# Weights in 16 pieces that alternate with activation tiles in one DMA queue, and an order planned for it

## The chip, the core and the metric

The kernel runs on one core of one Trainium2 chip. The core has a matrix engine (TensorE, PE in the profile; its weight loads are PEld), a vector engine (VectorE, DVE), an activation engine (ScalarE, ACT), GpSimd (POOL) and SyncE (SP). Here SP and POOL mostly issue DMAs: each has a queue of its own, and both queues are served by the same 16 DMA engines. The profile calls SP's queue q1 (hardware_dynamic) and POOL's queue q0 (software_dynamic).

The metric is the device time of one execution in microseconds (us); lower is better. Before the change it was 177.68 us, the median of 3 runs from 177.03 to 177.84.

## What is computed

An RWKV-like linear attention, followed by a two-layer network with squared ReLU. Cut to what matters:

```python
# r, k, v: (4, 8, 768, 48) f32   w, u: (8, 48)   w_in: (384, 2048)   w_out: (2048, 384)
for t in range(S):
    cur = einsum('bhd,bhe->bhde', u * k_t, v_t)
    y_t = einsum('bhd,bhde->bhe', r_t, state + cur)
    state = w[..., None] * state + einsum('bhd,bhe->bhde', k_t, v_t)
x = y.transpose(0, 2, 1, 3).reshape(3072, 384)
h = x @ w_in
out = (relu(h) ** 2) @ w_out
```

## The kernel before

The 768 positions are cut into 6 chunks of 128, and each chunk of each of the 4 batches is a unit: unit i is chunk i // 4 of batch i % 4, 24 units in all. For one unit the steps are these, with the engine that runs each:

- `load:i:rt`, `load:i:kt`, `load:i:vt`: DMAs of the r, k and v tiles, 192 KB each, in rows of 192 bytes. Buffers are taken in turn from small pools (`room`: 3 for r, 8 for k, 4 for v), so a load waits until the buffer's last reader is done.
- `scale:i:0` and `scale:i:1` (DVE): r and k times powers of the decay w, to bf16. `cast_v:i` (ACT): v to bf16.
- `turn:i:0/1` (PE) and `evict_rk:i:0/1` (ACT) transpose both for units 0 to 5; from unit 6 on one transposing DMA of SP's queue does it (`turn_dma:i`).
- `at:i` (PE) multiplies the two; `mask:i:0/1` (DVE) masks the product. `rk:i` (DVE) and `sums:i` (PE) make the diagonal term and the change of the state, `state_add`, `state_decay` (DVE) and `state_cast` (ACT) carry the state.
- `y_mm:i` (PE) and `evict_y:i` (DVE) give the attention's output. It is transposed by `x_turn:i` (PE) and `evict_x:i` (ACT) for units 0 to 5, by `x_dma:i` (SP's queue) after that.
- `mm1:i:m:s` (PE) is the first layer for one unit (m = 1, units 0 to 7) or two (m = 2), for slice s of the 2048 columns; `relu` (ACT) and `square` (ACT or DVE) follow. `mm2:i:q` (PE) is quarter q of the second layer's sum, `evict_o:i` (ACT) and `store:i` write the output.

The weights lie in SBUF in quarters: `w_in_q[0..3]` and `w_out_q[0..3]`, cast from f32 to bf16 by the DMA, which only POOL's queue is used for. A quarter is 768 KB in HBM and 384 KB in SBUF; one DMA brings one quarter (`weights:after:q:I` or `weights:after:q:O`). While units are single, slice s of `mm1` reads quarter s of `w_in` alone; `mm2:i:q` reads quarter q of `w_out` alone.

`fill` is a matmul of ones into a bank that nobody reads (68 of them): it keeps PE occupied where the plan has nothing for it.

The order of the work is written out: `SCHEDULE` is one list of steps, made by a planner from costs and due times, and each engine executes its own steps in the list's order. Nothing overtakes: if a step waits, all that stands behind it on its engine waits too. The two DMA queues are filled in the list's order as well. In each queue the program has eight completion semaphores in turn, so the ninth DMA is issued only when the first has landed, the tenth when the second has, and so on.

Before the change SP's queue brings the tiles of units 0 and 1, then k of units 6, 9 and 7, r of unit 6 and so on; POOL's queue brings the two small tiles of w and u (`columns`), the tiles of units 2 to 5 and the eight quarters of weights. POOL also computes the identity for the transposes (`identb`), the triangular mask (`smask`), and small products of the decay (`u_columns`, `end_columns`).

Of the kernel before, what the change touches and what calls it, by code (L numbers as in the profile page):

```python
# [11 lines left out]
ALU = mybir.AluOpType  # L12
# [10 lines left out]
2*fill sums:0@3 load:4:rt fill diag_v:0 turn:2:0@4 end_columns rk:1 at:1@6,7 evict_rk:2:0 evict_y:0 2*fill scale:2:1
2*fill x_turn:0@5 mask:1:1 6*fill mask:1:0 3*fill turn:2:1@1 scale:3:0 fill weights:-:3:I evict_rk:2:1 3*fill
scale:3:1 2*fill evict_x:0 fill turn:3:0@4 load:5:rt rk:2 cast_v:2 fill at:2@2,7 load:6:rt fill mask:2:0 fill
weights:-:0:O fill mm1:0:1:0@6 state_add:0 load:4:kt turn:3:1@1 relu:0:1:0 3*fill mask:2:1 fill cast_v:1 mm1:0:1:1@5
weights:-:1:O evict_rk:3:0 sums:1@2 state_cast:0 fill load:4:vt diag_v:1 sums:2@3 y_mm:1@6 relu:0:1:1 y_mm:2@7
evict_y:1 fill mm1:0:1:2@4 evict_rk:3:1 load:5:vt diag_v:2 fill rk:3 x_turn:1@5 at:3@6,1 evict_x:1 evict_y:2
load:5:kt fill relu:0:1:2 fill mask:3:0 3*fill cast_v:3 mm1:1:1:1@5 square:0:1:1:0 square:0:1:0:1 load:8:kt sums:3@7
mask:3:1 x_turn:2@4 mm1:1:1:0@6 evict_x:2 diag_v:3 relu:1:1:1 y_mm:3@1 state_add:1 weights:-:2:O mm1:2:1:2@4  # L30
relu:1:1:0 square:0:1:2:1 evict_y:3 mm1:2:1:1@5 square:1:1:0:1 state_add:3 weights:-:3:O mm1:2:1:0@6 state_add:2
x_turn:3@2 fill evict_x:3 mm1:2:1:3@1 scale:4:0 relu:2:1:2 fill mm1:1:1:3@7 relu:2:1:1 square:2:1:2:1 square:2:1:1:0
mm1:0:1:3@3 relu:2:1:0 mm1:3:1:1@2 square:2:1:0:1 mm1:3:1:3@4 relu:3:1:1 scale:4:1 mm2:1:0@5 square:1:1:1:1
relu:1:1:3 turn:4:0@6 mm2:0:0@2 relu:0:1:3 load:7:rt mm1:1:1:2@7 relu:2:1:3 evict_rk:4:0 fill turn:4:1@3 fill
mm1:3:1:0@1 evict_rk:4:1 cast_v:4 rk:4 mm2:1:1 scale:5:0 relu:1:1:2 at:4@6,0 relu:3:1:0 mm2:2:0@3 mask:4:1
state_cast:2 turn:5:0@7 mask:4:0 sums:4@1 square:1:1:2:1 mm2:0:1 scale:5:1 evict_rk:5:0 diag_v:4 y_mm:4@0 mm2:2:1
evict_y:4 turn:5:1@6 scale:6:1 mm2:0:2 evict_rk:5:1 state_add:4 square:3:1:0:1 x_turn:4@7 mm2:2:2 square:0:1:3:0
evict_x:4 square:3:1:1:1 at:5@0,6 load:6:vt mm2:3:0@1 state_cast:3 mask:5:1 mm1:4:1:0@7 square:1:1:3:0 load:8:rt
state_cast:1 rk:5 mm2:3:1 cast_v:5 mask:5:0 relu:3:1:3 mm2:0:3 square:2:1:3:0 mm1:4:1:3@6 scale:6:0 mm2:2:3
relu:4:1:3 turn_dma:6 relu:4:1:0 sums:5@0 y_mm:5@4 diag_v:5 mm1:4:1:2@6 load:8:vt scale:7:1 evict_y:5 mm1:4:1:1@7  # L40
relu:4:1:2 scale:7:0 square:4:1:0:1 mm2:1:2 state_decay:4 turn_dma:7 square:4:1:3:0 x_turn:5@4 mm2:1:3 evict_x:5
square:3:1:3:0 relu:4:1:1 mm2:4:0@6 load:7:vt evict_o:0 square:4:1:1:0 mm1:5:1:3@4 store:0:POOL load:9:rt scale:8:0
mm2:4:1 relu:5:1:3 scale:8:1 load:10:rt evict_o:1 rk:6 at:6@7,2 square:4:1:2:1 mm1:5:1:1@4 mask:6:1 cast_v:6
turn_dma:8 mm1:5:1:0@5 mask:6:0 relu:5:1:1 state_add:5 mm2:4:2 relu:5:1:0 square:5:1:1:1 mm1:5:1:2@2 sums:6@4
relu:5:1:2 mm2:4:3 diag_v:6 square:5:1:0:1 state_decay:5 y_mm:6@7 cast_v:7 rk:7 at:7@5,0 evict_y:6 square:5:1:2:1
mm2:5:0@2 mask:7:1 x_dma:6 mm1:3:1:2@7 state_add:6 mm2:5:1 relu:3:1:2 load:10:kt mask:7:0 load:9:vt sums:7@0
square:3:1:2:1 scale:9:1 mm2:5:2 evict_o:4 diag_v:7 y_mm:7@4 state_cast:4 store:4:POOL scale:9:0 at:8@7,5 evict_y:7
cast_v:8 turn_dma:9 mm2:3:2 store:1:POOL rk:8 mm1:6:1:0@6 square:5:1:3:0 x_dma:7 scale:10:0 sums:8@4 relu:6:1:0
mm2:5:3 state_add:7 mm1:6:1:1@6 evict_o:5 load:11:kt state_decay:6 square:6:1:0:1 mask:8:1 load:11:rt mm1:6:1:3@0
state_cast:5 scale:10:1 mm2:6:0@2 mask:8:0 state_cast:6 mm2:3:3 diag_v:8 turn_dma:10 relu:6:1:1 y_mm:8@5 relu:6:1:3  # L50
mm1:6:1:2@7 evict_y:8 cast_v:9 square:6:1:1:0 x_dma:8 at:9@6,0 relu:6:1:2 mm1:7:1:1@5 rk:9 square:6:1:2:1
square:6:1:3:0 sums:9@7 load:12:rt evict_o:2 mm2:6:1 mask:9:1 relu:7:1:1 load:10:vt store:2:POOL mask:9:0 mm2:6:2
store:5:POOL state_add:9 mm1:7:1:0@3 y_mm:9@0 diag_v:9 relu:7:1:0 mm1:7:1:3@5 scale:11:1 square:7:1:1:1 evict_y:9
mm1:7:1:2@6 evict_o:3 scale:11:0 square:7:1:0:1 x_dma:9 store:3:POOL mm2:6:3 relu:7:1:3 mm2:7:0@7 relu:7:1:2
square:7:1:3:0 turn_dma:11 at:10@3,0 square:7:1:2:1 state_decay:7 mm2:7:1 rk:10 mask:10:1 load:11:vt mm2:7:2
mask:10:0 load:12:kt cast_v:10 mm2:7:3 state_add:8 state_cast:7 load:13:kt sums:10@1 mm1:8:2:0@5 evict_o:6
state_decay:8 load:12:vt diag_v:10 state_cast:8 y_mm:10@6 mm1:8:2:1@0 evict_y:10 relu:8:2:0 state_decay:9
mm1:8:2:6@3 x_dma:10 relu:8:2:1 rk:11 scale:12:0 state_cast:9 at:11@4,2 mm1:8:2:2@6 mask:11:0 load:13:rt cast_v:11
mm1:8:2:5@5 square:8:2:0:1 mask:11:1 relu:8:2:2 mm1:8:2:3@0 scale:12:1 relu:8:2:6 square:8:2:1:0 turn_dma:12
sums:11@4 square:8:2:2:1 mm1:8:2:4@2 diag_v:11 relu:8:2:3 scale:13:1 mm2:8:0@6 load:14:rt relu:8:2:5 square:8:2:3:0  # L60
y_mm:11@3 square:8:2:6:1 mm2:9:0@0 evict_y:11 relu:8:2:4 scale:13:0 mm2:9:1 x_dma:11 square:8:2:5:1 state_add:11
cast_v:12 mm2:8:1 square:8:2:4:1 turn_dma:13 mm1:8:2:7@5 mm2:8:2 relu:8:2:7 load:14:kt mm2:9:2 square:8:2:7:0
load:13:vt at:12@3,2 rk:12 mm2:8:3 mask:12:1 load:15:kt sums:12@4 mask:12:0 evict_o:8 mm1:10:2:0@5 store:8:POOL
load:15:rt state_decay:11 state_add:10 y_mm:12@2 relu:10:2:0 store:6:POOL mm1:10:2:1@6 square:10:2:0:1 rk:13
load:16:rt mm1:10:2:3@3 diag_v:12 relu:10:2:1 evict_y:12 mm1:10:2:2@5 scale:14:0 x_dma:12 at:13@1,6 relu:10:2:2
square:10:2:1:0 mm1:10:2:4@2 relu:10:2:3 scale:14:1 cast_v:13 mm1:10:2:6@5 square:10:2:3:0 turn_dma:14 mm2:9:3
relu:10:2:6 mask:13:1 relu:10:2:4 sums:13@3 mask:13:0 mm1:10:2:7@5 load:14:vt square:10:2:2:1 scale:15:1
mm1:10:2:5@6 square:10:2:4:1 diag_v:13 evict_o:7 y_mm:13@2 relu:10:2:7 store:7:POOL mm2:10:0@1 evict_y:13
relu:10:2:5 scale:15:0 mm2:11:0@7 square:10:2:6:1 state_add:12 mm2:11:1 square:10:2:5:1 square:10:2:7:0 x_dma:13
mm2:10:1 state_decay:12 mm2:10:2 turn_dma:15 rk:14 at:14@5,2 state_decay:10 mm2:10:3 mask:14:1 state_cast:10  # L70
load:16:kt mm2:11:2 mask:14:0 cast_v:14 load:15:vt evict_o:9 mm1:12:2:0@6 state_add:13 load:17:rt state_cast:12
store:9:POOL y_mm:14@4 load:17:kt scale:16:0 sums:14@2 relu:12:2:0 mm1:12:2:1@5 diag_v:14 state_cast:11 mm1:12:2:2@0
evict_y:14 relu:12:2:1 state_add:14 x_dma:14 at:15@3,6 square:12:2:0:1 mm1:12:2:7@4 rk:15 state_decay:13
mm1:12:2:3@5 relu:12:2:7 scale:16:1 relu:12:2:2 mask:15:0 mm1:12:2:5@2 turn_dma:16 square:12:2:2:1 mask:15:1
mm2:11:3 cast_v:15 square:12:2:1:0 load:16:vt mm1:12:2:6@4 relu:12:2:3 state_decay:14 sums:15@0 square:12:2:3:0
relu:12:2:6 y_mm:15@3 load:18:rt evict_o:10 mm2:12:0@6 diag_v:15 state_cast:14 store:10:POOL state_add:15
mm1:12:2:4@5 relu:12:2:5 evict_y:15 mm2:13:0@4 relu:12:2:4 scale:17:0 x_dma:15 mm2:13:1 square:12:2:5:1 scale:17:1
# [39 lines left out]
def kernel(  # L117
# [440 lines left out]
```

## Time and profile before

| What | Time |
|---|---|
| Median of 3 runs | 177.68 us (177.03 to 177.84) |
| The profiled execution's own time | 176.95 us |
| Its span on the core | 175.1 us |
| PE busy | 167.7 us (96%) |
| DVE, ACT busy | 128.8 us (74%), 128.1 us (73%) |
| POOL busy, DMA issues among it | 33.2 us (19%) |
| First matmul, first `mm1` | 1.19 us, 18.06 us |
| SP's queue q1 | 18.88 MB in 89472 packets, 63.5% of 16 engines' span |
| POOL's queue q0 | 9.64 MB in 4352 packets, 22.7% |

The span counts from the core's first instruction to its last; 1.85 us of the execution's own time lie around it. Bytes are counted as written, so weights count at bf16. A line such as L447 is a line of the kernel before: L245 `fill`, L300 `scale`, L304 `cast_v`, L337 `at`, L447 `mm1`, L471 `mm2`, L278 `load`, L288 and L291 `weights`, L309 `turn_dma`, L424 `x_dma`.

### The profile page before, as it was taken

What the parts mean: (1) busy time and instruction counts of PE and PEld (TensorE: products, weight loads), DVE (VectorE), ACT (ScalarE), POOL (GpSimd) and SP (SyncE); (2) the same over time, 40 slices, a digit from 0 to 9 for tenths busy, and PEclk for the clock granted to TensorE, in tenths of its full rate; (3) what the DMA queues carried; (4) which work ended last, traced back from release to release, by engine and by line L of the source; (5) the groups of instructions that cost most, each with busy time, mean ns of one, the idle gap of its engine ahead of it and who ended that gap; (6) DMA issues with size and microseconds to landing.
All of it is one profiled execution on the core that took longest, in us unless ns stands there. A gap on an engine that the chain in (4) does not pass through costs nothing.

```text
span 175.1 us, 4846 instructions
## 1 busy us (share of the span) xinstructions
PE 167.7 (96%) x1946; PEld 132.1 (75%) x1946; DVE 128.8 (74%) x280; ACT 128.1 (73%) x266; POOL 33.2 (19%) x66
## 2 busy tenths in 40 slices
PE   7869999999999999999999999999999999999992
PEld 3547999777787888696786886986886886878870
DVE  4459797199788998997998999689988497550400
ACT  4344798977787797799486989299498595992951
POOL 8998560000010203000201101010110011120010
PEclk9999999999999999999999999999999999999999
DMA  5999999978595999999999998998999987521013
GB/s 109 196 221 191 215 231 249 197 139 160 108 217 106 193 159 215 198 196 155 178 236 170 230 118 188 205 131 190 207 172 170 161 165 201 112 78 35 4 45 135
DMA packets 93848, 28.83 MB, mean 165 GB/s; under 512 B 89681, under 2 KB 91730, under 8 KB 93826
## 3 DMA queue, kind: packets, MB, share of 16 engines
q1 hardware_dynamic: 89472, 18.88, 63.5%
q0 software_dynamic: 4352, 9.64, 22.7%
q8 instruction: 15, 0.25, 0.6%
q14 instruction: 7, 0.06, 0.2%
q10 hardware_dynamic: 2, 0.00, 0.0%
HBM read 20.45 MB, written 4.72 MB: 144 GB/s over the span
## 4 chain that ended last, share of the span: by engine, by line
PE 76%; DMA 9%; ACT 6%; DVE 4%; SPq 2%; issue 1%; DVEq 0%
PE bank L447 31%; PE bank L471 30%; DMA ldv<-in_v_dram 4%; PE bank L337 4%; DMA rkT<-rkw 3%; PE bank L245 2%; PE bank L400 2%; PE bank L362 2%; ACT gr L455 2%; DMA xT<-yb 2%; SPq L278 2%; PE bank L406 2%; PE bank L486 2%; ACT g L462 1%; DVE g L464 1%; ACT osb L478 1%
## 5 line engine op out<-in xcount | busy, mean ns | idle before, releaser
L447 PE MATMUL bank<-xT,w_in_q 128*128 128x128 bf16 (+1 forms) x768 | 72.4, 246 | 0.3 <-DMA xT<-yb 0.3
L455 ACT ACTIVATE gr<-bank 128x512 f32<-128x512 f32 x96 | 53.7, 603 | 20.2 <-PE bank L447 18.9
L471 PE MATMUL bank<-w_out_q,g 128*128 128x384 bf16 x368 | 68.5, 326 | 0.0
L447 PEld LDWEIGHTS <-w_in_q 128*128 128x128 bf16 x768 | 64.1, 114 | 3.6 <-issue 0.5
L471 PEld LDWEIGHTS <-g 128*128 128x128 bf16 x368 | 33.5, 98 | 18.4
L462 ACT ACTIVATE g<-gr 128x512 bf16<-128x512 f32 x60 | 37.0, 641 | 0.4
L505 POOL DMA_DIRECT2D out_dram<-osb x21 | 11.3, 542 | 131.5 <-ACT osb L478 120.3
L349 DVE TENSOR_TENSOR am<-bank,smask 128x512 bf16<-128x512 f32 x48 | 31.5, 683 | 1.9 <-PE bank L337 1.5
L464 DVE TENSOR_TENSOR g<-gr 128x512 bf16<-128x512 f32 x36 | 24.5, 685 | 9.9 <-ACT gr L455 9.7
L371 DVE TENSOR_TENSOR dv<-vb,bank 128x384 f32<-128x384 bf16 x24 | 13.2, 549 | 7.5 <-PE bank L362 4.6
L300 DVE TENSOR_TENSOR rkw<-ldr,wpos 128x384 bf16<-128x384 f32 x24 | 13.2, 551 | 5.2 <-DMA ldr<-in_r_dram 2.6
L415 DVE TENSOR_TENSOR yb<-bank,dv 128x384 bf16<-128x384 f32 x24 | 13.3, 554 | 4.8 <-PE bank L406 4.1
L391 ACT CAST stb<-st 64x192 bf16<-64x192 f32 x40 | 13.9, 349 | 2.4 <-DVE st L385 2.0
L304 ACT CAST vb<-ldv 128x384 bf16<-128x384 f32 x24 | 12.3, 513 | 3.8 <-DMA ldv<-in_v_dram 3.5
L478 ACT COPY osb<-bank 128x384 f32<-128x384 f32 x23 | 11.0, 486 | 5.5 <-PE bank L471 5.4
L245 PE MATMUL bank<-warm 128*128 128x256 bf16 x68 | 13.6, 315 | 1.2 <-DVE warm L193 1.2
L329 DVE TENSOR_TENSOR rk<-rkT 128x512 bf16<-128x512 bf16 x24 | 10.0, 419 | 5.8 <-ACT rkT L324 4.3
L300 DVE TENSOR_TENSOR rkw<-ldk,wneg 128x384 bf16<-128x384 f32 x24 | 13.2, 550 | 0.3 <-DMA ldk<-in_k_dram 0.3
L381 DVE TENSOR_TENSOR st<-bank,st 64x192 f32<-64x192 f32 x32 | 11.2, 351 | 0.2
L324 ACT COPY rkT<-bank 128x512 bf16<-128x512 bf16 x12 | 6.9, 585 | 6.0 <-PE bank L320 5.9
L400 PE MATMUL bank<-vb,am 128*128 128x48 bf16 x192 | 8.6, 183 | 1.4 <-ACT vb L304 1.4
L400 PEld LDWEIGHTS <-am 128*128 128x128 bf16 x192 | 7.8, 96 | 2.6 <-issue 1.4
(61 smaller groups left out, 115.6 us busy)
## 6 DMA issues: line engine op xcount, KB each, us to landing
out_dram<-osb POOLq DMA_DIRECT2D x21, 192.0 KB, 3.3
ldk<-in_k_dram SPq DMA_DIRECT2D x20, 192.0 KB, 4.0
ldr<-in_r_dram SPq DMA_DIRECT2D x20, 192.0 KB, 4.1
ldv<-in_v_dram SPq DMA_DIRECT2D x20, 192.0 KB, 4.0
w_in_q<-in_moe_w_in_dram POOLq DMA_DIRECT2D x4, 384.0 KB, 8.6
w_out_q<-in_moe_w_out_dram POOLq DMA_DIRECT2D x4, 384.0 KB, 11.4
ldr<-in_r_dram POOLq DMA_DIRECT2D x4, 192.0 KB, 8.4
ldk<-in_k_dram POOLq DMA_DIRECT2D x4, 192.0 KB, 8.7
```

The costliest lines, as they stand in the source:

```text
L245: nc.tensor.matmul(out=bank("fill")[:, :WIDE], lhsT=warm[:, :128], rhs=warm, start=True, stop=True)
L300: nc.vector.tensor_tensor(t["rkw"][:, x, :, :, :D], pair(src), pair(wx), ALU.mult)
L349: nc.vector.tensor_tensor(am, t["at"][o], smask.unsqueeze(1).to_broadcast([C, HP, C]), ALU.mult)
L371: nc.vector.tensor_tensor(t["dv"], t["vb"], t["d"].unsqueeze(2).to_broadcast([C, H, D]), ALU.mult)
L391: nc.scalar.copy(stb[b][sl, :, o * D : (o + 1) * D], st32[b][sl])
L400: nc.tensor.matmul(out=y[:, 2 * p + o, :], lhsT=t[f"am{o}"][:, p, :], rhs=t["vb"][:, 2 * p + o, :], start=(o == 0 and p == 0), stop=c == 0 ...
L415: nc.vector.tensor_tensor(t["yb"], t["y"], t["dv"].rearrange("p h d -> p (h d)"), ALU.add)
L447: nc.tensor.matmul(out=t["h", s][:, a], lhsT=turned, rhs=chunks[c]["xT"][:, n, b : b + m, :], start=(n == 0), stop=(n == NK - 1),)
L455: nc.scalar.activation(t["gr", s], t["h", s], AF.Relu)
L462: nc.scalar.activation(g, x, AF.Square)
L464: nc.vector.tensor_tensor(g, x, x, ALU.mult)
L471: nc.tensor.matmul(out=t["o"], lhsT=chunks[units[i][0]]["g"][:, f, units[i][1], :], rhs=w_out_q[f // 4][:, f % 4, :], start=(f == 0), stop ...
```

## The change

- Each quarter of `w_in` comes in two DMAs (rows 0 and 1 of three, then row 2: two thirds and one third), each quarter of `w_out` in two halves: 16 DMAs instead of 8. The gate that held the first quarter back until k of unit 0 had landed is gone.
- POOL's queue also takes r and k of unit 1 and v of units 0 and 1, so that it brings 16 tiles and 16 pieces, alternating. SP's queue keeps r and k of unit 0, takes the small tiles of w and u, and goes on with units 6 and 7.
- The identity and the mask become steps (`identity`, `triangle`) that stand between POOL's DMAs; the memset of `uwb`, `u_columns` (3 instructions) and `end_columns` (7) move from POOL to DVE.
- 5 buffers for r instead of 3, 6 for k instead of 8.
- A new `SCHEDULE` for all engines. It has the same steps otherwise, 68 `fill` among them.

The start of POOL's queue in the new order, I and O naming `w_in` and `w_out`, a and b the first and the second piece in the array's order: r2, r1, I0a, k1, v0, k2, I0b, k3, I1a, v1, I2b, r3, I1b, v2, I2a, v3, I3b, r4, I3a, r5, O1a, k4, O1b, k5, O0a, O0b, v4, O3b, O2b, v5, O2a, O3a. SP's queue: r0, k0, w, u, r6, k6, r7, k7, r8, v6, then the first `turn_dma`.

```diff
 SCHEDULE = """
-load:0:kt fill@0 load:0:rt 2*fill load:1:rt 2*fill load:1:kt fill columns 2*fill spread_log@1 load:0:vt load:2:rt
-load:1:vt weights:kt.0:0:I fill power:0 3*fill load:2:kt power:1 scale:0:0 load:6:kt fill spread_columns@2 scale:1:0
+load:0:rt fill@0 load:0:kt load:2:rt 2*fill columns 2*fill load:1:rt 3*fill spread_log@1 weights:0:I:0 identity
+load:1:kt fill power:0 2*fill load:0:vt fill power:1 scale:0:0 3*fill scale:0:1 load:2:kt spread_columns@2 load:6:rt
...
-    room = {'ldr': 3,
-            'ldk': 8,
+    room = {'ldr': 5,
+            'ldk': 6,
...
-    make_identity(nc, identb)
...
-    make_upper_triangular(nc, smask, val=1.0, diag=False)
...
-    nc.gpsimd.memset(uwb, 0.0)
+    nc.vector.memset(uwb, 0.0)
...
     def columns():
-        nc.gpsimd.dma_start(out=wu[:, 0, :, :D], in_=w.rearrange("(p o) d -> p o d", o=2))
-        nc.gpsimd.dma_start(out=wu[:, 1, :, :D], in_=u.rearrange("(p o) d -> p o d", o=2))
+        nc.sync.dma_start(out=wu[:, 0, :, :D], in_=w.rearrange("(p o) d -> p o d", o=2))
+        nc.sync.dma_start(out=wu[:, 1, :, :D], in_=u.rearrange("(p o) d -> p o d", o=2))
+
+    def identity():
+        make_identity(nc, identb)
+
+    def triangle():
+        make_upper_triangular(nc, smask, val=1.0, diag=False)
...
     def u_columns():
-        nc.gpsimd.tensor_tensor(cols[:, 1, :], cols[:, 1, :], cols[:, 0, :], ALU.mult)
+        nc.vector.tensor_tensor(cols[:, 1, :], cols[:, 1, :], cols[:, 0, :], ALU.mult)
...
-        (nc.gpsimd if i in (2, 3, 4, 5) else nc.sync).dma_start(
+        (nc.gpsimd if i in (1, 2, 3, 4, 5) or (name == "vt" and i in (0, 1)) else nc.sync).dma_start(
...
-    def weights(after, q, which):
-        if after is not None:
-            nc.gpsimd.tensor_copy(gate, tiles[after[1]][after[0]][:, 0, :1])
+    def weights(q, which, part):
         if which == "I":
             src = moe_w_in.rearrange("(ko ki) f -> ki ko f", ki=128)
-            nc.gpsimd.dma_start(out=w_in_q[q], in_=src[:, :, q * dff // NQ : (q + 1) * dff // NQ])
+            sl = slice(0, 2) if part == 0 else slice(2, NK)
+            nc.gpsimd.dma_start(out=w_in_q[q][:, sl, :], in_=src[:, sl, q * dff // NQ : (q + 1) * dff // NQ])
         else:
             src = moe_w_out.rearrange("(q ki a) d -> q ki a d", q=NQ, a=NF // NQ)
-            nc.gpsimd.dma_start(out=w_out_q[q], in_=src[q])
+            sl = slice(2 * part, 2 * part + 2)
+            nc.gpsimd.dma_start(out=w_out_q[q][:, sl, :], in_=src[q][:, sl, :])
```

The parts of the new order that the prediction speaks of, PE's steps alone, with n f for n `fill`:

```
before: 8f spread_log 5f spread_columns 3f turn:0:0 1f turn:0:1 2f turn:1:0 1f at:0 2f turn:1:1 3f y_mm:0 2f
        sums:0 1f turn:2:0 at:1 4f x_turn:0 9f turn:2:1 7f turn:3:0 1f at:2 3f mm1:0:1:0 ...
after:  8f spread_log 7f spread_columns 1f turn:0:0 3f turn:0:1 4f turn:1:0 1f at:0 3f turn:1:1 sums:0 y_mm:0 1f
        at:1 5f turn:2:0 8f x_turn:0 12f turn:2:1 2f sums:1 2f mm1:0:1:0 y_mm:1 at:2 turn:3:0 mm1:0:1:1 ...
        mm2:1:0 mm2:0:0 y_mm:4 sums:4 mm2:0:1 mm2:1:1 turn:5:1 mm1:3:1:3 1f mm2:1:2 at:5 ...
```

In ACT's new order `evict_x:0` stands behind `evict_rk:2:0` and `cast_v:1`.

More of the change, by code (lines that the diff above doesn't have):

```diff
@@ L23 @@
[L23 to L77, printed above, removed]
@@ L509 @@
         at, cast_v, columns, copy_columns, diag_v, end_columns, evict_half, evict_o,
[L510 to L513 removed]
+        evict_rk, evict_x, evict_y, fill, identity, load, mask, mm1,
+        mm2, mm2_half, power, relu, rk, scale, spread_columns, spread_log,
+        square, state_add, state_cast, state_decay, store, store_half, sums, triangle,
+        turn, turn_dma, u_columns, weights, x_dma, x_turn, y_mm
     )}
```

142 lines of the change are left out of this document (97 added, 45 removed).

## The prediction

> **What bounds the kernel now.** I read the page's busy line first, then the stretches before and after the first `mm1`, then the chain of waits, then the DMA queues, then POOL's order in time.
>
> ```profile
> PE 167.7 (96%) x1946; PEld 132.1 (75%) x1946; DVE 128.8 (74%) x280; ACT 128.1 (73%) x266; POOL 33.2 (19%) x66
> ```
> ```profile
> 0.00:18.06 18.06, 14.58 (x127) 9.74 (x128) 11.04 (x37) 7.47 (x13) 16.59 (x38) 1.00 1.04 179
> 18.06:171.60 153.54, 153.15 (x1821) 122.40 (x1819) 117.71 (x244) 120.12 (x252) 16.57 (x29) 1.00 0.86 163
> ```
>
> PE is the bound. From its first `mm1` at 18.06 us to its end at 171.6 it idles 153.54 - 153.15 = 0.39 us; before 18.06 it idles 18.06 - 14.58 = 3.48 us, of which 1.19 us lie before its first matmul.
>
> ```profile
> 4.06 7.81 DMA ldv<-in_v_dram
> 11.89 0.51 ACT vb L304
> ...
> 14.29 0.48 DVE yb L415
> ...
> 18.23 0.67 PE bank L447 x12
> ...
> 134.50 0.56 DVE rkw L300
> 135.11 5.00 DMA rkT<-rkw
> 140.16 0.40 PE bank L337 x8
> ...
> 155.71 3.23 DMA xT<-yb
> 158.98 3.44 PE bank L447 x30
> ```
>
> The chain of waits starts with v of unit 0, 7.81 us on its way in SP's queue; all of PE's later work is shifted by it. Later it leaves PE twice, for two transposing DMAs (5.00 and 3.23 us).
>
> ```profile
> q0 software_dynamic: 1276, 2.91, 95.3%
> q1 hardware_dynamic: 1286, 0.24, 14.8%
> ```
>
> This is the DMA view from 20 to 34 us. Both queues have work, and they send the same number of packets; q0's are 2281 bytes on average, q1's 187. So SP's queue crawls while POOL's is full: v of unit 1 needed 13.5 us, k of units 6, 9 and 7 about 23.
>
> ```profile
> 3.63 0.96 POOL L278 DMA_DIRECT2D ldr<-in_r_dram  x1
> 23.35 0.88 POOL L278 DMA_DIRECT2D ldk<-in_k_dram  x1
> 25.23 0.56 POOL L291 DMA_DIRECT2D w_out_q<-in_moe_w_out_dram  x1 [0.99 <-DMA w_in_q<-in_moe_w_in_dram]
> 25.98 0.55 POOL L291 DMA_DIRECT2D w_out_q<-in_moe_w_out_dram  x1 [0.20 <-issue]
> ```
>
> This is POOL in order of time. Its first tile, r of unit 2, was issued at 3.63 and landed 4.95 us later, at 8.6. Quarter 2 of `w_out` waited for a DMA eight places ahead and landed 10.7 us after its issue, at 35.9; quarter 3 came at 37.9.
>
> **PE's own work.** Both kernels give PE the same steps, so I add up PE's steps in each order as if nothing ever waited: `fill` 0.21 us cold (8 in 1.89) and 0.11 from about 10.3 us on (9 in 0.98), `turn` 0.43 and 0.22, `at` 0.44 (0.33 and a hole of 0.1 ahead), `sums` 0.27, `y_mm` 0.20 (0.37 from unit 4), `x_turn` 0.17, `mm1` 0.67, `mm2` 0.65. Both walks end at 168.0. The real end was 171.6, so waits cost 3.6 us: 2.45 before the first `mm1` (walk 15.6, real 18.06) and 1.1 after it. A gain can come from these 3.6 us alone. What counts is the shift, real time less walk: it is a maximum over late arrivals, so a later wait costs only what the earlier ones have not paid.
>
> **Part 1, the first tiles in POOL's queue and first in line.** POOL's first DMA can go out at about 1.25, behind the identity of 4x4 and the iota (1.10 to 1.22) rather than at 3.63. Its first tile then lands near 6.2 by the same 4.95 us. From landings (16.2 to 33.5 us: 5 quarters, 7 tiles; 11.3 to 37.9 less the first 4.9 us: 7 and 7) a quarter costs 2.21 us and a tile 0.90; an issue of a tile costs POOL 0.91. So r1 comes at 7.1, I0a at 8.6, k1 at 9.5, v0 at 10.4, I0b at 12.0, and, three tiles, I1a and the rest further, v1 at 15.3. Two tiles issued early came 1.2 apart, so v1 may be as late as 16.5.
>
> Walk with these: w and u follow two tiles in SP's queue (tiles landed at 3.82 and 5.14 there) and come near 6, as now (6.4). `turn:0:0` runs at 6.9, `at:0` at 9.8. DVE has ten more small instructions; its copy of 8 columns took 0.16 us, so ten cost 1.3 to 1.6 us, and `scale:1:1` and both masks queue behind them: `turn:1:1` at 10.9 rather than 10.5. v0's cast ends at 10.9, not 12.4, and `y_mm:0` ends near 12.4, `x_turn:0` near 14.6 (now 14.82). `evict_x:0` waits on ACT behind v1's cast: 15.3 + 0.51 + 0.48 = 16.3. The first `mm1` then runs at 17.0, a shift of 1.2 instead of 2.45. Bounds: 16.6 (v1 a microsecond early, with DVE's chain then the limit) and 18.2 (v1 at 16.5, and v2 and the rest with it).
>
> **Part 2, the weights' end.** What POOL's queue must bring ahead of O2a, the piece that `mm2:1:2` starts with: after r2, 15 tiles at 0.90, four quarters of `w_in` at 2.21, seven halves of `w_out` at 1.10, each with 0.08 for the smaller packets: 13.5 + 8.8 + 8.3 = 30.6. With 6.2 that is 36.8; I add 0.5 for the first tiles, and take 37.3. Bounds: the same sum for the kernel before gives 34.0 where 35.9 was measured, so up to 38.7; below, 35.8, if the first tile lands a microsecond sooner. The new order reaches `mm2:1:2` at 34.4 on the walk: 66 `fill` 9.9, 15 `mm1` 10.05, 4 `mm2` 2.6, 12 `turn` 3.3, 5 `at` 2.2, the rest and the start 6.3. So PE stands there until 37.3, a shift of 2.9 (1.4 to 4.3). `at:5`, `mm2:2:0` and all that follows stand behind it. Before, the first step with quarter 2 was `mm2:0:2`, walk 35.9, real 38.3: the piece had landed 2.4 us earlier. The others are milder: k4 near 27.3 for `turn:4:1` (walk 26.8; with its scaling 1.2), O0b near 31.6 for `mm2:1:0` (30.1), v4 near 32.5 and its cast for `y_mm:4` (31.4; 1.7).
>
> That the quarters come in pieces changes POOL's issue time by 8 issues of 0.57: nothing waits for it, since its DMAs go out eight landings ahead. If that cover were gone, 4.6 us.
>
> The Trainium skill, "DMA: Bandwidth & Descriptors", section "Issuing engines are not separate DMA queues", holds that all issuers share 16 engines, so moving loads saves only issue time. Here the DMA share is indeed 1.07 to 1.22 from 5 to 35 us, but the queues' equal packet counts show that the order of landing changes. By that rule alone v0 would still come at 11.9, and the shift at `mm2:1:2` would stay as above.
>
> **Part 3, the steady stage.** SP's queue brings r6, k6, r7, k7 at one packet per POOL packet. It is free of POOL's stream at about 37.5 with r8 and v6 left, so `turn_dma:6` can follow near 39 (43.86 now), and `at:6` has over 2 us to spare. After that the orders differ in the lead they give a transposing DMA, in PE time between its place and its use. Now units 12, 17, 20, 23 have 5.9, 6.5, 5.0, 4.4 before `at`; then 4.3, 3.9, 4.3, 3.7, and such a DMA took 3.2 to 5.9. For `x_dma` of 9, 11 and 21: 4.0, 4.0, 3.2 now, then 3.0, 3.0, 2.7, with 2.3 to 5.4 needed. The stage has cost 1.1 us; I take 1.5 (bounds 0.5 and 4). The last stores and the 3.5 us behind PE's end are the same steps.
>
> **Sum.** PE ends at 168.0 + 2.9 + 1.5 = 172.4 instead of 171.6: +0.8. Against the profiled execution: span 175.9, own time 177.8. That execution (176.95) lies 0.7 below the median of 177.68, so the forecast for a median is 178.5.
>
> **Rivals.**
> - *A, the forecast: the early gain is given back at O2a.* Its own range is 177.5 (shift 2.2 and 1.2) to 180 (shift 4.3 and 1.6).
> - *B, faster: the pieces are in time.* If the queue is 1.5 us ahead of my sum, O2a lands at 35.8 and the others with it: the largest shift left is 1.4, and with 1.2 after it PE ends at 170.6, giving 176.7. It decides where O2a lands before 36.2. For it: all DMA starts 2.4 us sooner on POOL, and r1, k1 no longer take turns with it. Against: four more tiles and half a quarter stand ahead of O2a. If every wait but 0.5 us went, 174.6.
> - *C, slower: the thinner leads.* `x_dma:9`, `x_dma:11` or a `turn_dma` comes 1 to 2 us late on top: PE ends near 174.5, 180.6.
> - *D, each DMA has a price of its own.* The POOL queue has 32 loads instead of 22. If each of ten more cost the 1.0 us between issue-limited tiles, O2a would land at 47 and the time be near 188. Against: tiles landed as little as 0.4 us apart behind a quarter, with eight in flight. The Trainium skill, same page, section "Anatomy of one DMA", states a fixed 2.0 us per DMA, which would be 20 us here if they did not overlap; by the landings they do.
>
> **How the numbers follow.** A 0.56, B 0.26, C 0.14, D 0.02, no effect at all 0.02. About 0.5% (0.9 us) is what a measurement of this kernel can tell from no change: 176.8 to 178.6. A, whose middle is 178.5, lies above 178.6 half the time (0.29) and inside otherwise (0.27); B, with 176.7, is faster in two cases of three (0.17), inside in the third (0.09). With C and D slower is 0.45; with no effect the same is 0.38; faster 0.17. The range leaves out D, half of C and the far end of B: 176.4 to 180.6.
>
> **What would show it.** Right: v of unit 0 lands before 11 and the first `mm1` starts near 17; PE then waits for a DMA of `w_out_q` at about 36 to 37, the only wait of over 0.5 us between 18 and 60. Wrong if no such wait stands there (B), if `mm1` starts after 18.2 (v1, or DVE's ten instructions, mispriced), or if a wait on rkT or xT over 1 us stands after 60 (C).

## The result and the profile after

The changed kernel takes 178.23 us (median of 20 executions, 177.54 to 179.18); the kernel before, measured beside it, 177.45 (20, 176.66 to 179.9). The ratio is 1.005, with a 95% interval of 1.0034 to 1.0066: slower by half a per cent. The forecast was 178.5.

The page of the kernel after, busy time of each engine:

```profile
PE 168.9 (96%) x1946; PEld 133.3 (76%) x1946; DVE 130.6 (74%) x291; ACT 128.2 (73%) x266; POOL 36.7 (21%) x64
```

Its stretches before and after the first `mm1` (us; busy time and instruction counts of PE, PEld, DVE, ACT and POOL; clock, DMA share, GB/s):

```profile
0.00:18.60 18.60, 15.99 (x129) 11.06 (x130) 12.20 (x47) 7.33 (x13) 15.43 (x29) 1.00 1.03 192
18.60:172.13 153.53, 152.90 (x1820) 122.22 (x1818) 118.43 (x244) 120.44 (x253) 21.27 (x36) 1.00 0.84 162
```

The first `mm1` starts at 18.60 instead of 18.06, and PE ends at 172.13 instead of 171.57; the span is 175.8 instead of 175.1. So the early gain that part 1 expected did not come, and the late loss was small. The page's PEclk shows full speed from the start in both kernels, but the rows do not: one `fill` takes about 0.21 us until 12 us here, 0.11 later.

PE's timeline of the kernel after (start, us, what, and in brackets the idle time before it and what ended it):

```profile
7.75 0.27 PE L263 MATMUL bank<-ident,wu 4*128 4x4 f32 x1 [1.17 <-DMA wu<-in_u_dram]
...
11.80 0.82 PE L250 MATMUL bank<-warm 128*128 128x256 bf16 x3
...
14.54 0.72 PE L250 MATMUL bank<-warm 128*128 128x256 bf16 x5
...
22.63 0.86 PE L452 MATMUL bank<-xT,w_in_q 128*128 128x128 bf16 x12 [0.46 <-DMA w_in_q<-in_moe_w_in_dram]
...
37.97 0.81 PE L476 MATMUL bank<-w_out_q,g 128*128 128x384 bf16 x4
```

PE waits for u (1.17 us at 7.75) and for the first piece of quarter 2 of `w_in` (0.46 us at 22.63, the step `mm1:0:1:2`). The row at 37.97 is `mm2:1:2`, where the prediction had PE stand for O2a: there is no wait before it. The chain of waits of the kernel after says the same:

```profile
5.62 0.76 POOL ldv L283
6.49 7.13 DMA ldk<-in_k_dram
13.90 0.88 POOL ldv L283
14.78 7.80 DMA w_in_q<-in_moe_w_in_dram
22.63 0.86 PE bank L452 x12
```

Before, it went through v of unit 0. Now it goes through POOL's queue twice: k of unit 2, 7.13 us on its way, lets POOL issue the next DMAs (eight are out at once), and I2a, issued at 14.78, lands at 22.58. With the prediction's ledger (real time less walk) the shift is 1.63 after u, 2.83 at the first `mm1`, 3.55 at `mm1:0:1:2`, and 4.12 at the end; before it was 2.45 and 3.58.

### The profile page after: what moved, and what is told of

It is laid out like the page before. It is cut to its first block, busy times and chain, and to the rows that moved or that the text cites. A ratio compares the mean times of both kernels' runs of the same rounds, so it can differ in the third digit from the quotient of the medians.

```text
span 175.8 us, 4872 instructions
## 1 busy us (share of the span) xinstructions
PE 168.9 (96%) x1946; PEld 133.3 (76%) x1946; DVE 130.6 (74%) x291; ACT 128.2 (73%) x266; POOL 36.7 (21%) x64
## 4 chain that ended last, share of the span: by engine, by line
PE 82%; DMA 10%; POOL 3%; ACT 1%; issue 1%; POOLq 0%
PE bank L452 36%; PE bank L476 32%; DMA w_in_q<-in_moe_w_in_dram 4%; DMA ldk<-in_k_dram 4%; PE bank L342 4%; PE bank L405 2%; DMA xT<-yb 2%; PE bank L411 2%; PE bank L367 2%; PE bank L491 2%; POOL ldr L283 1%; POOL ldv L283 1%; PE bank L362 1%; ACT gr L460 1%; PE bank L325 1%
## 5 line engine op out<-in xcount | busy, mean ns | idle before, releaser
L452 PE MATMUL bank<-xT,w_in_q 128*128 128x128 bf16 (+1 forms) x768 | 73.7, 246 | 0.6 <-DMA w_in_q<-in_moe_w_in_dram 0.5
L460 ACT ACTIVATE gr<-bank 128x512 f32<-128x512 f32 x96 | 55.0, 602 | 21.9 <-PE bank L452 21.6
L476 PE MATMUL bank<-w_out_q,g 128*128 128x384 bf16 x368 | 67.3, 326 | 0.0
L476 PEld LDWEIGHTS <-g 128*128 128x128 bf16 x368 | 34.3, 98 | 18.9
L467 ACT ACTIVATE g<-gr 128x512 bf16<-128x512 f32 x60 | 36.2, 633 | 0.6
L250 PEld LDWEIGHTS <-warm 128*128 128x128 bf16 x68 | 7.1, 115 | 3.9 <-issue 1.3
L342 PE MATMUL bank<-rkT 64*128 64x128 bf16 x192 | 9.7, 222 | 0.0
```

The costliest lines, as they stand in the source:

```text
L250: nc.tensor.matmul(out=bank("fill")[:, :WIDE], lhsT=warm[:, :128], rhs=warm, start=True, stop=True)
L342: nc.tensor.matmul(out=t["at"][o][:, p, :], lhsT=t["rkT"][sl, 1, p, :], rhs=t["rkT"][sl, 0, p, :], start=True, stop=True,)
L452: nc.tensor.matmul(out=t["h", s][:, a], lhsT=turned, rhs=chunks[c]["xT"][:, n, b : b + m, :], start=(n == 0), stop=(n == NK - 1),)
L460: nc.scalar.activation(t["gr", s], t["h", s], AF.Relu)
L467: nc.scalar.activation(g, x, AF.Square)
L476: nc.tensor.matmul(out=t["o"], lhsT=chunks[units[i][0]]["g"][:, f, units[i][1], :], rhs=w_out_q[f // 4][:, f % 4, :], start=(f == 0), stop ...
```

## Experiments

Two theories are tested throughout. P: the end is set by the pace of POOL's queue, which SP's tiles slow, through I2a at 22.6 us. S: it is set by the small waits of the start (u, DVE's instructions). D is the rival of the prediction, that each DMA has a price of its own; a theory formed on the way, called C in one expectation (not the prediction's rival C), is that PE's clock, released late, sets the end.

### w and u first in line

```diff
-load:0:rt fill@0 load:0:kt load:2:rt 2*fill columns 2*fill load:1:rt
+load:0:rt fill@0 columns load:0:kt load:2:rt 2*fill 2*fill load:1:rt
...
```

> The changed kernel with the two small tiles of w and u ahead of k of unit 0 in SyncE's queue. Measured in the changed kernel: PE waits 1.2 us for u at spread_columns (7.75), quarter 2 of w_in is whole at 22.58 and holds mm1:0:1:2, PE ends at 172.1. Theory P (the pace of POOL's queue sets the end): spread_columns starts near 6.4 and the first mm1 near 17.5, but the quarter still comes at 22.3 to 22.7, the wait there grows from 0.5 to about 1.5 us, and PE ends at 171.8 to 172.1: no more than 0.3 us gained. Rival S (the small waits at the start set the end): the 1.2 us stay gained, PE ends near 170.9.

Measured: 178.42 us, ratio 1.0079 (1.0053 to 1.0105). `spread_columns` ran at 6.32 us without a wait, and it was worth nothing: the clock stayed low until about 16.2 us, the first `mm1` ran at 19.53, I2a landed at 23.09, and PE ended at 172.85. All three lie later than P had them (17.5, 22.7 at most, 172.1); the late clock is a likely reason for the first, not a shown one. The time still decides against S: without the wait for u the kernel is no faster (178.23).

### SP's tiles of units 6 and 7 left out

```diff
     def load(i, name):
+        if i in (6, 7) and name != "vt":
+            return
...
+        if i in (6, 7):
+            t["kt"] = t["rt"] = wpos
```

> The changed kernel without the loads of r and k of units 6 and 7; a constant is read in their place, so the results from unit 6 on are other numbers. SyncE's queue is then empty beside POOL's stream. Theory P: POOL's stream loses its partner at one packet per packet, some 15 ns each: quarter 2 of w_in comes 1 to 2 us sooner, near 21, piece O2a near 36 instead of 37.7; the shift is then set by the start (2.8) and PE ends 0.5 to 0.8 us sooner, near 171.5. Rival S: the landings move by under 0.4 us or, where they move, PE's end stays within 0.2 us of 172.1.

Measured: 176.45 us, ratio 0.996 (0.9942 to 0.9979). I2a lands at 20.03 instead of 22.58, O2a at 34.54 instead of 37.73, v of unit 0 at 10.67 instead of 12.60. The shift after `mm1:0:1:2` is 2.25, none of it from a piece, and PE ends at 171.43, as P had it. Four tiles in the other queue were worth 2.5 us at I2a and 3.2 at O2a, more than expected.

### Whole quarters

Every quarter in one DMA again, in the place of its second piece:

```diff
+    seen = set()
...
+        if (q, which) not in seen:
+            seen.add((q, which))
+            return
...
-            sl = slice(0, 2) if part == 0 else slice(2, NK)
+            sl = slice(0, NK)
...
-            sl = slice(2 * part, 2 * part + 2)
+            sl = slice(0, 4)
```

> The changed kernel with whole quarters (8 DMAs), each at the place of its second piece in the order. Theory P: the bytes ahead of each whole quarter are the same, so quarter 2 of w_in lands at 22 to 22.6 and quarter 2 of w_out at 37 to 37.7 (seven fewer extra packets of 0.08 us); v of unit 0 comes near 11.2 instead of 12.6, since two thirds of a quarter stand behind it. PE ends at 171.7 to 172.1. Rival D (each DMA has a price of its own, 0.2 us or more): the quarters come 1.5 us sooner at O2 and the end is 0.7 us or more sooner.

Measured: 178.5 us, ratio 1.007 (1.0048 to 1.0093); five executions took 178.24 to 178.9, the sixth 584.27. The trace is that of one more execution of the same kernel:

> Same kernel as e3_whole_quarters (every quarter whole again, in the place of its second piece; nothing left out), for a trace. Its time was 178.5 us. Theory P (the pace of POOL's queue sets the end, through quarter 2 of w_in): quarter 2 lands near 22.3 us (the one execution seen so far had that, but was far longer as a whole), so the first mm1 that reads it stands 0.3 to 0.5 us and the shift after it is near 3.3; against the 22.58 of the changed kernel only 0.3 us is won, as 8 DMAs fewer (0.2 each, from the kernel before with pieces) are worth 0.8 to 1.0 us by then but the whole quarter also has to be complete at the place of its second piece. Theory D (each DMA has a price of 1.0 us): quarter 2 would land about 3 us earlier, near 19.5. PE's end 171.7 to 172.2 by P.

Measured: 178.01 us in the one execution. Quarter 2 landed at 22.94, later than I2a (22.58), not earlier; PE waited 0.55 us for quarter 1 and 0.88 for quarter 2, and ended at 172.60:

```profile
20.15 0.86 PE L457 MATMUL bank<-xT,w_in_q 128*128 128x128 bf16 x12 [0.55 <-DMA w_in_q<-in_moe_w_in_dram]
...
22.99 0.86 PE L457 MATMUL bank<-xT,w_in_q 128*128 128x128 bf16 x12 [0.88 <-DMA w_in_q<-in_moe_w_in_dram]
```

D's 19.5 is excluded. In the new order the cut itself is not what made the kernel slower: without it the ratio is 1.007 against 1.005, in intervals that overlap.

### The kernel before, with pieces alone

```diff
-            nc.gpsimd.dma_start(out=w_out_q[q], in_=src[q])
+            for sl in (slice(0, 2), slice(2, 4)):
+                nc.gpsimd.dma_start(out=w_out_q[q][:, sl, :], in_=src[q][:, sl, :])
```

and the same for `w_in`, with rows 0 and 1 and then row 2.

> The kernel before with each quarter in its two pieces, one right behind the other, nothing else changed. Theory P: the landings of the second pieces differ by under 0.5 us from the quarters' (24.9 for quarter 3 of w_in, 35.9 for quarter 2 of w_out), as they are not the last to arrive for PE; its end stays at 171.6 within 0.3 us, ratio 1.000 within 0.002. Rival D: 8 more DMAs at 0.2 us or more make the last quarter come after 39.5; since eight in flight are now fewer bytes, POOL's issues also come later, and the end is 0.5 us or more later.

Measured: 177.79 us, ratio 1.0029 (1.0013 to 1.0044). The second pieces land later than the whole quarters did, by 0.4 us for the first, 1.3 for the second and 1.1 to 1.7 for the other six. By the last that is 1.7 us for eight more DMAs, 0.2 each: a price, a fifth of D's 1.0, and more than the 0.08 of the prediction. The expectation under P (landings within 0.5 us, ratio within 0.002) was missed; the sign that it named for D with a price of 0.2, a last quarter after 39.5, was met (39.66, and PE's end at 172.36).

### `end_columns` back on POOL

```diff
-        nc.vector.tensor_tensor(wend_c, cols[:, 0, :], cols[:, 0, :], ALU.mult)
+        nc.gpsimd.tensor_tensor(wend_c, cols[:, 0, :], cols[:, 0, :], ALU.mult)
...
-            nc.vector.tensor_tensor(wend_c, wend_c, wend_c, ALU.mult)
+            nc.gpsimd.tensor_tensor(wend_c, wend_c, wend_c, ALU.mult)
```

> The changed kernel with end_columns (7 small instructions) back on POOL. Theory P: turn:1:1 and what follows come up to 0.5 us earlier (in the changed kernel scale:1:1 stood behind end_columns on DVE until 12.08 us), but I2a sets the shift later (3.55 us), so the end does not move; 7 instructions of 0.1 to 0.2 us on POOL delay the DMAs behind them by up to 1 us only if POOL has no slack: the DMAs go out when a landing 8 places ahead releases them, so they have. Time 178.0 to 178.6, ratio to the kernel before 1.002 to 1.008. Theory S (the small waits of the start set the end): 0.5 us faster, near 177.7. If POOL's issues are late, I2a lands later and the time is up to 179.

Measured: 179.62 us, ratio 1.013 (1.0084 to 1.0176): a miss. POOL's timeline of this run:

```profile
10.08 0.36 POOL L275 TENSOR_TENSOR wend_c<-cols 128x4 f32<-128x4 f32 x1
10.52 1.97 POOL L277 TENSOR_TENSOR wend_c<-wend_c 128x4 f32<-128x4 f32 x6
12.43 0.91 POOL L283 DMA_DIRECT2D ldv<-in_v_dram  x1
```

The seven products take 2.35 us on POOL (1.3 on DVE), and v of unit 1, which the changed kernel issued at 10.06, goes out at 12.43 and lands at 18.91 instead of 17.55; I2a lands at 23.30. The expectation had POOL with slack there; it had none, since enough landings lay behind it and the DMA waited for POOL alone. Its 0.1 to 0.2 us an instruction was wrong too: in the kernel before the same seven took 2.42 us on POOL (13.42 to 15.84). A late issue that makes I2a late fits P, started from POOL's side. The clock played a part too: released at about 10.1 us, it was low again from 13.5 to 16.9, after PE had waited 1.25 us for `turn:1:1`. How much each part cost was not separated. Nor does this trace explain the median: three of the six executions took 178.12 to 178.82, the profiled one (178.63) among them, and three 180.42 to 180.66, of which there is no trace.

### SP's tiles moved behind the weights

```diff
-        (nc.gpsimd if i in (1, 2, 3, 4, 5) or (name == "vt" and i in (0, 1)) else nc.sync).dma_start(
+        (nc.gpsimd if i in (1, 2, 3, 4, 5) or (name == "vt" and i in (0, 1)) or (name != "vt" and i in (6, 7)) else nc.sync).dma_start(
```

In `SCHEDULE` the end of POOL's queue becomes v4 O2b v5 O2a r6 k6 O3b r7 O3a k7, and `scale:6:0` stands directly ahead of `scale:6:1`. All four tiles stand behind O2a, and so does O3b, which stood ahead of it; nothing ahead of I2a in POOL's queue changes.

> The changed kernel with r and k of units 6 and 7 moved from SP's queue to the end of POOL's (among and behind the last pieces); SP's queue goes on with r of unit 8 and v of unit 6; scaling of unit 6's k stands directly ahead of that of its r on DVE. Nothing is left out. Theory P: as in the run in which these four tiles were not loaded at all, I2a lands near 20.0 us (22.58 in the changed kernel), O2a near 34.5 to 35.5 (37.73), the shift of PE after the start stays near 2.3 and PE ends near 171.4; time 176.3 to 177.0, ratio 0.994 to 0.999. The four tiles now land between 36 and 40 us on POOL, and turn_dma:6 follows near 40 as now. Theory D (each DMA on POOL has a price): O2a would be 2 us later than without the tiles. Theory S (waits at the start alone): no change from 178.2. Risk: unit 6's or 7's scaling comes late and a turn_dma with it; then PE waits for at:6 after 45 us, by 1 us or more.

Measured: 176.35 us, ratio 0.996 (0.9939 to 0.9981): faster than both kernels. The DMA view from 8 to 23 us of the kernel after (packets, MB, share of 16 engines' time):

```profile
q0 software_dynamic: 1719, 2.83, 91.2%
q1 hardware_dynamic: 2910, 0.55, 25.6%
```

The same view of the kernel before:

```profile
q0 software_dynamic: 1796, 2.58, 91.2%
q1 hardware_dynamic: 2656, 0.50, 27.5%
```

The same view of this run:

```profile
q0 software_dynamic: 2011, 3.10, 107.4%
q1 hardware_dynamic: 43, 0.01, 0.4%
```

In the changed kernel SP's queue moves 0.55 MB in these 15 us, with 1.69 packets for each of POOL's, and POOL's moves 2.83. With SP quiet POOL's moves 3.10; from 5 to 8 us it is 0.64 instead of 0.37. The view of `w_in`'s tiles in the kernel after (the first row gives the issues and their duration in ns, the second the time from issue to landing):

```profile
L292 POOL DMA_DIRECT2D w_in_q<-in_moe_w_in_dram x8: 558/652/742, 3.5 to 19.0; - x8
...
DMA to landing us min/median/max: 5.9/7.3/7.8
```

The same view of this run:

```profile
L197 POOL DMA_DIRECT2D w_in_q<-in_moe_w_in_dram x8: 578/674/786, 3.5 to 16.9; - x8
...
DMA to landing us min/median/max: 4.1/4.8/6.1
```

I2a lands at 19.17, O2a at 34.36, r and k of units 6 and 7 between 35.5 and 39.5, and the first `turn_dma` goes out at 39.18 (39.88). That O2a comes no later than with the four tiles left out (34.54) is no test of D here, since one piece fewer stands ahead of it. PE's stretches of this run, before and after its first `mm1`:

```profile
0.00:18.06 18.06, 15.76 (x128) 10.76 (x129) 12.17 (x47) 7.59 (x14) 16.93 (x31) 1.00 0.96 192
18.06:171.65 153.59, 153.03 (x1820) 122.06 (x1818) 118.28 (x244) 120.13 (x253) 23.45 (x38) 1.00 0.82 163
```

The same bytes through the same 16 engines, in another order of landing, are worth 0.9% (1.005 to 0.996). The profiled pair shows only part of it, 172.13 against 171.65 at PE's end: the profiled execution of the changed kernel (177.54) was its fastest of 20, this one's (176.79) near the top of its 7. `mm1:0:1:2` starts 1.13 us sooner here (21.50), but later PE waits 0.56 us in all for two of the transposing `x_dma`, in the changed kernel 0.16 for one.

### More `fill`

```diff
-spread_columns@2
+6*fill spread_columns@2
...
-turn:1:1@1
+3*fill turn:1:1@1
...
-sums:0@2
+2*fill sums:0@2
```

> The changed kernel with 11 more fill matmuls in places where PE stood idle: 6 ahead of spread_columns, 3 ahead of turn:1:1, 2 ahead of sums:0. Nothing is left out. Theory C (PE's idle stretches put off the release of the full clock, seen at 9.7 us in the kernel before, 13.5 in the changed kernel): release near 10.1 us, and 0.5 to 0.7 us of the cold steps come back at y_mm:0 and x_turn:0; the first mm1 runs near 18.0 to 18.3 rather than 18.6. If C also sets the end, time near 177.6. Theory P: the end does not move, since I2a at 22.6 sets 3.55 us of shift whatever PE did before: PE's end near 172.1, time 178.0 to 178.5, ratio 1.002 to 1.007.

Measured: 178.46 us, ratio 1.0055 (1.0033 to 1.0076). The clock was released at about 7.7 us and the first `mm1` ran at 18.19. The timeline of this run, PE's rows:

```profile
22.39 0.86 PE L357 MATMUL bank<-xT,w_in_q 128*128 128x128 bf16 x12
...
153.15 0.23 PEld L247 LDWEIGHTS <-rkT 64*128 64x128 bf16 x8 [1.14 <-DMA rkT<-rkw]
```

I2a landed at 22.35 and `mm1:0:1:2` stands at 22.39. With the clock released 5.8 us earlier, and the added `fill` on PE, the first `mm1` came 0.4 us sooner, `mm1:0:1:2` 0.2, and the time is the same: P, not the clock. PE's end (173.11) lies 0.98 later than in the changed kernel's profiled execution, and most of that is a wait near the end. The second row is the weight load of `at:23`, which waits 1.14 us for the transposing DMA of unit 23 (issued at 148.24, as in the changed kernel at 148.15, where `at:23` ran at 152.18 with next to no wait). Here the prediction's rival C is to be seen, on a small scale: a thin lead, and a DMA that took over 4 us. Two of the eight executions took 177.4 to 177.5, the other six 178.35 to 178.64, so such a wait might come and go; and since the profiled execution of the changed kernel was its fastest, the usual one might hold it.

### A longer lead for unit 23

This is what the last run tests:

```diff
-scale:23:1 mm2:19:1 x_dma:21 store:14:POOL
+scale:23:1 scale:23:0 mm2:19:1 x_dma:21 turn_dma:23 store:14:POOL
```

> The changed kernel with one thing moved: scaling of unit 23's r directly behind that of its k on DVE, and its transposing DMA directly behind x_dma:21 in SP's queue, so that it goes out near 146.8 us instead of 148.15. Nothing is left out. In the run with more fill at:23 waited 0.9 to 1.1 us for this DMA; in the profiled execution of the changed kernel, its fastest of 20, it did not. Theory T (the usual execution of the changed kernel pays that wait, which is rival C of the prediction on a small scale): the median falls by 0.5 to 0.9 us, to 177.3 to 177.7, ratio 1.000 to 1.003. Theory P alone (the loss is all in the first 23 us): 178.0 to 178.4, ratio 1.003 to 1.007, with at:23 unmoved in a profiled execution that has no wait there.

Measured: 178.21 us, ratio 1.0051 (1.0033 to 1.0069), the same as the changed kernel. The DMA went out at 147.42 and `at:23` did not wait, so T falls. This profiled execution, unlike that of the changed kernel, is a usual one (178.21). PE's timeline:

```profile
20.77 0.40 PE L324 MATMUL bank<-identb,rkw 128*128 128x128 bf16 x4 [1.02 <-DVE rkw L304]
...
22.92 0.83 PE L451 MATMUL bank<-xT,w_in_q 128*128 128x128 bf16 x12
```

The first row is `turn:3:0`: it waits for the scaling of r of unit 3, whose tile lands on POOL at 20.13, 2.1 us behind the piece ahead of it (19.12 in the changed kernel's profiled execution, 16.70 with SP's tiles moved). I2a landed at 22.81. The shift after `mm1:0:1:2` is 3.84 and PE ends at 172.80. r of unit 3 is late in the other runs with SP's tiles in place too: 19.61 with more `fill`, 20.44 with w and u first, 19.99 in the kernel with the earlier start alone (below). So the profiled execution of the changed kernel is the exception, and in the usual one another transfer of the same queue stands in front. That this is the same cause, P, is argued from the landings.

### An earlier start, with and without SP's tiles

Both kernels have this edit, the first on the kernel with the tiles moved, the second on the changed kernel (in the last pair PE's steps alone):

```diff
-turn:1:0@5 end_columns fill load:1:vt
+turn:1:0@5 fill load:1:vt
...
-evict_y:0
+evict_y:0 end_columns
...
-8*fill x_turn:0
+4*fill x_turn:0
```

Six more `fill` are gone between `x_turn:0` and `turn:2:1`.

> The kernel e6_sp_tiles_behind with, besides, end_columns on DVE behind evict_y:0 instead of ahead of scale:1:1 (1.28 us of small instructions) and ten fill matmuls fewer between turn:2:0 and turn:2:1 (four ahead of x_turn:0, six behind it). Nothing is left out. Theory P: in e6 the pieces had landed 2 us ahead of the steps that read them, so PE was set by its own start there (shift 2.3 to 2.6); with 1.1 us of fills gone and turn:1:1 no longer waiting for DVE (0.2 us) and y_mm:0 for the masks (0.3), everything up to the first mm1 moves up by 1.1 to 1.6 us, I2a (19.2) is still in time for mm1:0:1:2 near 20.2, and v of unit 4 (31.95, needed near 32.2 to 32.7 with its cast) is the next in line. PE's end 170.1 to 170.8, time 174.9 to 175.9, ratio 0.987 to 0.993. Against: v of unit 1 (15.4) and evict_x:0 behind its cast, then the first mm1 would stay at 17.5 or later and the gain is 0.5. Rival: fewer fills keep the clock low for longer, and the start is not faster at all (176.3).

Measured: 176.31 us, ratio 0.9948 (0.9927 to 0.997), no different from 176.35. The first `mm1` ran at 16.68, 1.4 us earlier, as expected; then PE waited for the next thing in line:

```profile
18.03 0.37 PE L404 MATMUL bank<-vb,am 128*128 128x48 bf16 x8 [0.51 <-DVE am L353]
```

This is unit 1's mask on DVE. `mm1:0:1:2` came at 21.11 (21.50), and PE's end at 171.55 (171.65), with waits of 0.45 and 0.52 us for `x_dma` at 64.00 and 148.49. Time and PE's end missed the expectation (175.9 and 170.8 at most): its list of late arrivals behind the first `mm1` had DMAs alone and left out this mask.

> The changed kernel with the two edits of e8_earlier_start alone (end_columns later on DVE, ten fills fewer), SP's queue as in the changed kernel. Nothing is left out. Theory P: quarter 2's first piece lands at 22.3 to 22.6 as before, so mm1:0:1:2 waits for it by 1.1 to 2 us and PE's end stays where it was: 171.9 to 172.6, time 177.9 to 178.6, ratio 1.002 to 1.008. Theory S (the start's own waits set the end): 1.1 to 1.6 us faster than the changed kernel, near 176.8.

Measured: 178.51 us, ratio 1.0083 (1.0064 to 1.0102). With SP's tiles in place the same edit gains nothing even at the first `mm1` (18.66). ACT's timeline of this run:

```profile
12.80 0.51 ACT L307 CAST vb<-ldv 128x384 bf16<-128x384 f32 x1 [1.89 <-DMA ldv<-in_v_dram]
...
17.71 0.51 ACT L307 CAST vb<-ldv 128x384 bf16<-128x384 f32 x1 [1.89 <-DMA ldv<-in_v_dram]
18.13 0.47 ACT L438 COPY xT<-bank 128x384 bf16<-128x384 bf16 x1
```

`evict_x:0`, the last row, stands behind the cast of v of unit 1 and ends at 18.60; the first `mm1` follows at 18.66. `mm1:0:1:2` then runs at 22.82, when I2a has landed (22.77). PE's end, 172.89, is 0.3 us above P's range. S is refuted twice, here and by the time with w and u first.

### The kernel before, with its tiles moved

```diff
-        (nc.gpsimd if i in (2, 3, 4, 5) else nc.sync).dma_start(
+        (nc.gpsimd if i in (2, 3, 4, 5) or (i, name) in ((6, "rt"), (6, "kt"), (7, "kt"), (9, "kt")) else nc.sync).dma_start(
```

> The kernel before, with k and r of unit 6 and k of units 7 and 9 moved from SP's queue to POOL's, ahead of, between and behind the last two quarters, and k of unit 8 behind r of unit 8 in SP's queue. Nothing is left out. It tells whether the time below both kernels that e6_sp_tiles_behind has (176.35) belongs to these tiles alone. Theory P for the kernel before: quarters and tiles on POOL land 2 to 3 us sooner from 20 us on, but v of unit 0, the transfer that set its shift (2.45 us at the first mm1), is in SP's queue and comes at most 1 us sooner, as v of unit 1 stays behind it; what is left is up to 0.5 us at the first mm1 and 0.4 at the steps from 21 us on. Time 176.8 to 177.4, ratio 0.997 to 1.000. If the tiles alone were the whole gain: 176.3 to 176.5. Risk: unit 6's scaling, a place earlier in DVE's order than its tiles now land, stalls DVE; then slower, up to 178.

Measured: 177.22 us, ratio 1.0012 (0.9995 to 1.0029): no gain. v of unit 0 landed at 9.11 instead of 11.87, and the first `mm1` still ran at 17.91 (18.06): u, now 7.25 instead of 6.62, and DVE's mask and output of unit 0 took its place. The steady stage then cost 2.2 us instead of 1.1 in the profiled execution, the slowest of the 12 (178.09); PE waits 0.39 us ahead of `at:9` and 0.51 ahead of `at:20`. So this run does not show cleanly what the tiles are worth there. It does show that moving them is not by itself the gain of 176.35.

## Why the prediction came out

- **The frame held.** PE's work is the same in both orders (walk 168.0) and the end is a maximum over late arrivals: 168.0 + 4.12 against the forecast 172.4. The size, +0.8 us, is what the medians show (178.23 - 177.45). But the terms were others: 2.83 by the first `mm1` where 1.2 was forecast, 3.55 by 23 us where 2.9 was forecast at 37, and less in the steady stage. A largest early shift that was 0.65 us worse and a steady stage that was 0.93 us better than forecast nearly cancel, so it is luck that the sum fits so well. Of rival A's mechanism, an early gain given back at O2a, neither half was seen; two of the three signs of being wrong that the prediction named were there (no wait at 36 to 37 us, first `mm1` after 18.2).
- **Part 1, the early gain (first `mm1` at 17.0, bounds 16.6 to 18.2), failed: 18.60.** The first tile came as forecast (6.07 against 6.2), then everything behind it late: k1 11.47 against 9.5, v0 12.60 against 10.4, v1 17.55 against 15.3 (16.5 at most). The mechanism was the one named, `evict_x:0` behind v1's cast, in ACT's timeline of the changed kernel:

```profile
17.57 0.51 ACT L309 CAST vb<-ldv 128x384 bf16<-128x384 f32 x1 [1.47 <-DMA ldv<-in_v_dram]
17.98 0.47 ACT L440 COPY xT<-bank 128x384 bf16<-128x384 bf16 x1
```

  Only the landing was mis-sized. The prices of 2.21 us a quarter and 0.90 a tile were means over 11 to 38 us, and SP's queue was taken to send one packet for each of POOL's, as it does from 20 to 34 us in the kernel before. From 8 to 23 us it takes 1.69 (1.48 in the kernel before, where the same view was there to be read). With SP quiet the forecast landings came nearly true: v0 10.04, v1 15.42, in the kernel with the tiles moved.
- **w and u "near 6, as now" failed.** u ended a wait at 7.75. It was issued on SP at 2.75, behind two tiles there and with POOL's first already out. In four other runs with the same place in SP's queue and SP's tiles behind it, its wait ended at 6.93 to 7.23, without these tiles at 6.95 to 7.09, so the 7.75 is also a matter of the execution. First in line it cost no wait, which changed nothing in the end.
- **The clock was not in the sum.** The walk let `fill` be short from 10.3 us on; in the changed kernel that came at about 13.5. By the run with more `fill` that was worth 0.4 us at most at the first `mm1`, and nothing at the end.
- **Part 2, the shift at O2a (landing at 37.3, shift 2.9), had the right landing and the wrong place.** O2a landed at 37.73. PE was already 3.55 late by then, through I2a, and `mm2:1:2` started at 37.97 without waiting. By the prediction's own prices I2a would have come at 21.0 (6.2, 8 tiles at 0.90, three pieces at 1.47 and three at 0.74, six times 0.08, and 0.5), a shift of 1.9, less than O2a's but more than any of the milder ones that the prediction lists; I2a is missing from its list. It came at 22.58. So the sign that the prediction named, a wait at 36 to 37 us, is absent, and the loss came 15 us earlier. O2a's sum was close because SP's share is largest at the start and falls (in the changed kernel 3.1 packets for each of POOL's from 5 to 8 us, 1.69 from 8 to 23, 1.16 from 20 to 34): the mean price is right over 30 us and wrong over 15.
- **The price of a piece (0.08 us) was too low:** no run shows it; in the kernel before it was 0.2. POOL's issue time is hidden only where the queue waits for landings: with `end_columns` on POOL v of unit 1 was issued 2.4 us later and landed 1.4 us later.
- **Part 3, the steady stage (1.5 us): 0.57** in the profiled execution (1.1 before); `turn_dma:6` came at 39.88, as forecast. The thin leads cost nothing that this trace shows; the 1.14 us ahead of `at:23` in one run is the most that was seen of that rival, and a longer lead there won nothing.
- **The rivals.** B, faster, needed O2a before 36.2; the kernels where that happened (34.54, 34.36) were faster, but only with SP's tiles out of the way. D, with its 1.0 us, is excluded by the whole quarters and by the price of 0.2.
- **The rule that the prediction cites.** The Trainium skill, "DMA: Bandwidth & Descriptors", section "Issuing engines are not separate DMA queues", holds that all issuers share the engines and that using more of them saves issue time. The traces agree that they share: POOL's queue moved 3.10 MB instead of 2.83 from 8 to 23 us when SP's moved 0.01 instead of 0.55. They disagree that only issue time is at stake: four tiles moved from one queue to the end of the other brought I2a 3.4 us forward and the time down by 0.9%.

What stays open: of the 0.78 us between the medians the two profiled executions show 0.56 at PE's end and 0.14 behind it. The profiled execution of the changed kernel was its fastest; what its usual one looks like is inferred from the run with the longer lead, which differs by one step, and from r3's landings in three others. PE's end with SP's tiles moved lies 0.48 us below the changed kernel's profiled execution and 1.15 below that run's, while the medians differ by 1.88; the rest is not traced. Why r3 and I2a land some tenths earlier or later from one execution to the next was not traced.

## What to carry to other kernels

A mean landing price holds only for the mix of queues over which it was taken: read packets and bytes of every queue in the stretch where the early, binding transfers run, not over the whole load phase. Then make the list of late arrivals complete, each load with its first reader and the engines' own chains too, since the one that binds is a maximum and the next is close behind. In the changed kernel tiles wanted at 40 us shared the engines with pieces wanted at 20; behind the urgent loads in the other queue they cost nothing. In the kernel before, where u and DVE's mask then held the start, such a move won nothing (177.22).

## What the runs showed of the hardware

- A small DMA is slow when tiles are out ahead of it: u (1.5 KB, issued at 2.75 us) ended a wait at 7.75 us in the changed kernel and at 6.93 to 7.23 in seven near-identical ones; first in line, issued at 2.17, it was there by 6.32.
- The full clock came at very different times: about 9.7 us in the kernel before, 13.5 after, 16.2 with w and u first, 7.7 with more `fill`; once, with `end_columns` on POOL, it was taken back for 3.4 us (13.47 to 16.89). The Trainium skill, "TensorE: Matmul & The Clock Gate", section "Part 1: The HAM clock gate (the "warmup" mystery)", tells of a window of about 3.4 us that runs freely; the 3.4 us of that one run agree with it. That `fill` in the idle places hastens the release is what one trace suggests; chance of phase was not excluded.
- Seven products of 128x4 numbers took 2.35 us on POOL and 1.3 us on DVE, and while POOL ran them it issued no DMA.
